# Attention and Fourier mixing on one core: new prices and smaller allowances in a planner

## The chip, the core and the metric

One of the eight cores of a Trainium2 chip runs the kernel. The metric is device time in microseconds (us) for one execution. The engines are TensorE (PE, matmuls; PEld, its weight loads), VectorE (DVE), ScalarE (ACT), GpSimd (POOL) and SyncE (SP, which here only issues DMAs). Each works through its own instructions in their written order and waits on semaphores for the others.

## The reference

Two independent parts, side by side in the output (2048 x 2048, fp32):

```python
# A: multi-head attention, S = 2048, D = 1024, 32 heads of 32
qkv = (x @ wqkv).reshape(B, S, 3, H, Dh).transpose(2, 0, 3, 1, 4)
scores = einsum("bhqd,bhkd->bhqk", q, k) * Dh ** -0.5
o = einsum("bhqk,bhkd->bhqd", softmax(scores), v)
a_out = o.transpose(0, 2, 1, 3).reshape(B, S, D) @ wo
# B: Fourier mixing by dense matrices, S = 2048, D = 1024
a = einsum("bsd,ed->bse", x, dft_hid_re);  b = einsum("bsd,ed->bse", x, dft_hid_im)
y = einsum("ts,bse->bte", dft_seq_re, a) - einsum("ts,bse->bte", dft_seq_im, b)
out = concatenate([a_out, y], axis=-1)
```

## The kernel before, in words

**Dense products (`fills`).** The projections of A and both steps of B are computed by a seven-product scheme on half-size blocks: each dense product is seven block products of sums and differences of blocks. The steps are `qkv` (A's projections), `dense1` and `dense2` (B), `project` (A's last product). An operand is loaded by SP (`fetch`, L380 for the first block, L389 for those added to it), summed on POOL or DVE (L396), and split by `halves` in a high part (a cast, L416 on ACT or L418 on DVE) and a low part (a subtraction, L421 on POOL or DVE). `group` then issues 12 or 24 matmuls (L332: high x high, low x high, high x low over 4 or 8 chunks) into one PSUM bank, and DVE evacuates the bank: in `qkv` L564 and L566, in the later steps L766 to L786. In `qkv`'s product 7 each group ends in two evacuations, each of which also adds a partial result `c` that SP loads back from DRAM (L643); partial results are stored there by L668 and L679. Sums used again are stored too: `sq_d`, `t1x_d` and others at L405. The fills have one fixed order. There are 6720 of them, 168 for each of the first five steps of `qkv`; product 7 is fills 1440 to 1727.

**Attention (`streams`).** For each head, stream S computes scores by rows (L1069, two matmuls into a double bank `psS`); DVE takes the negated row maximum (L1075), and ACT the exponentials with their sums (L1078). Stream T computes the transposed scores (L1201) with the maxima as further rows, and ACT writes their exponentials `pt` (L1205). Stream V multiplies four rows of `pt` with V (L1219: 16 products into a bank of `psD`, 32 PE instructions), and DVE adds them up in `ot` (L1230, L1232). Small products with `ident` (L1103, L1152) turn maxima and sums; `result` multiplies by the inverse sums (L1247, POOL or DVE).

**What sets the order.** At build time `Plan` plays the run through with a price for each operation, and every engine's instructions are written in the order in which the plan starts them. On the chip nothing of the plan's clock remains, only the orders. The main loop is PE's: at each moment it takes the next fill or the head of S, T or V, whichever is ready and ranks first; a head of a stream or the first matmul of a group must have been ready for `LATE` us. `others` starts what is ready on ACT, DVE, POOL and SP in order of rank; an operation with an `other` engine goes to whichever of the two is free first. The times:

```python
    def after(self, d, e, o):
        return d.end + (self.LAT_PE if e == "PE" else self.LAT) + self.SLACK.get((e, o.engine), 0.0)
...
                t = max(self.free[e], self.lane[0])
                self.dma = max(self.dma, t) + o.kb / o.lanes / self.KB_US
                o.end = self.dma + self.LANDING
```

So a transfer that SP starts to issue (price `ISSUE`, 0.46 us) is taken to move at `KB_US` KB per us behind all earlier ones, to land `LANDING` us later, and to be there for engine X another 0.1 + `SLACK[SP, X]` us later. `SLACK` thus keeps an engine from being given work that would make it stand and wait for a late transfer. `begin` holds SP back while `dma` is more than `QUEUE` ahead. A row-score operation costs 2 `MM`, a fill or transposed score `MM`, a product with V `SWITCH + 4 PV`.

Of the kernel before, what the change touches and what calls it, by code (L numbers as in the profile page):

```python
# [60 lines left out]
class Plan:  # L61
# [5 lines left out]
    LAT_PE = 0.2  # L67
    OVERLAP = {"ACT": 0.13, "DVE": 0.08, "POOL": 0.08}

    SLACK = {("SP", "POOL"): 2.0, ("SP", "DVE"): 2.5, ("SP", "PE"): 2.0, ("POOL", "DVE"): 0.7}  # L70
    KB_US = 340.0
    LANDING = 1.8
    QUEUE = 1.0

    def __init__(self):
# [37 lines left out]
    def after(self, d, e, o):  # L113
        return d.end + (self.LAT_PE if e == "PE" else self.LAT) + self.SLACK.get((e, o.engine), 0.0)

# [7 lines left out]
    def start(self, o, e=None):  # L123
# [4 lines left out]
        if o.kb:  # L128
            for _ in range(o.lanes):
# [3 lines that stand above are left out]
                self.lane = self.lane[1:] + [o.end]  # L133
# [52 lines left out]
def kernel(  # L186
# [90 lines left out]

    MM, PV, SWITCH, TINY = 0.232, 0.87, 0.34, 0.25  # L280
    ES, ET = 1.22, 0.61
    MAX, EVAC, CAST, BIT = 1.22, 0.69, 0.45, 0.27
    SUB = 1.34
    ISSUE = 0.46

    LATE = 0.3
    HB = 0
    ACAST = 0.6
    RES = 600
# [988 lines left out]
    while nf < len(fills) or any(place[n] < len(s) for n, s in streams.items()):  # L1278
# [18 lines left out]
        for n, (o, h, k) in heads.items():  # L1297
            if o.left:
                continue
            ready = o.ready + LATE  # L1300
            if n == "V":
# [4 lines left out]
            if n == "V":  # L1306

                near = any(m in heads and heads[m][0].left == 0 and heads[m][0].ready + LATE < pl.now + NEAR and not (m == "S" and held) for m in "ST")
                if (near or stock < STOCK) and pl.now < o.ready + PATIENCE:
# [14 lines left out]
        if nf < len(fills):  # L1324
            o, first, left = fills[nf]
            ready = o.ready if o.left == 0 else 1e18
            if first:
                ready = max(ready, room)
            if ready + (LATE if first else 0.0) <= pl.now:
                fill = o  # L1330
            elif ready < 1e17:
                times.append(ready + LATE)
        if fill is not None and (not ok or (not first and left <= HB) or nf / (FILL - RES) <= done / ATT):
# [56 lines left out]
```

## Time and profile before

| | |
|---|---|
| median of 3 runs | 3121.78 us (3120.04 to 3122.42) |
| the profiled execution | 3121.61 us |
| its span | 3119.8 us |
| granted clock of PE, mean | 0.994 |
| PE, DVE, ACT, POOL busy | 3066.8, 2503.5, 2299.1, 924.9 us |
| DMA | 567.77 MB, mean 182 GB/s |

The span runs from the first to the last instruction of the profiled execution; the time is taken outside it. Busy PE counts matmuls with their modelled ends, which overlap, so the distance from one start to the next tells more than the duration of one. The waits name the engine and tile that ended an idle time. In a row of a stretch the columns are its length, the busy us (and instructions) of each engine, the granted clock, the DMA share and GB/s.

### The profile page before, as it was taken

What the parts mean: (1) busy time and instruction counts of PE and PEld (TensorE: products, weight loads), DVE (VectorE), ACT (ScalarE), POOL (GpSimd) and SP (SyncE); (2) the same over time, 40 slices, a digit from 0 to 9 for tenths busy, and PEclk for the clock granted to TensorE, in tenths of its full rate; (3) what the DMA queues carried; (4) which work ended last, traced back from release to release, by engine and by line L of the source; (5) the groups of instructions that cost most, each with busy time, mean ns of one, the idle gap of its engine ahead of it and who ended that gap; (6) DMA issues with size and microseconds to landing.
All of it is one profiled execution on the core that took longest, in us unless ns stands there. A gap on an engine that the chain in (4) does not pass through costs nothing.

```text
span 3119.8 us, 45400 instructions
## 1 busy us (share of the span) xinstructions
PE 3066.8 (98%) x15040; PEld 2151.0 (69%) x15040; DVE 2503.5 (80%) x3182; ACT 2299.1 (74%) x4316; POOL 924.9 (30%) x683
## 2 busy tenths in 40 slices
PE   9899999899999999999999999999999999999999
PEld 7687666566666666666676666666666666666787
DVE  6669888878777878887777798888877888887886
ACT  4237888778888888888888878888888887775321
POOL 3423323412112321122111253323211244433443
PEclk9999999999999999999999999999999999999999
DMA  9975557876634544464433576445433467546952
GB/s 333 326 241 192 184 159 246 291 233 217 182 86 145 190 132 155 135 189 147 133 126 104 180 241 195 146 148 173 141 115 98 141 213 232 159 150 206 330 172 91
DMA packets 359673, 567.77 MB, mean 182 GB/s; under 512 B 86640, under 2 KB 88176, under 8 KB 359440
## 3 DMA queue, kind: packets, MB, share of 16 engines
q1 hardware_dynamic: 359440, 564.87, 56.8%
q8 instruction: 121, 1.98, 0.3%
q14 instruction: 112, 0.92, 0.1%
HBM read 407.70 MB, written 156.50 MB: 181 GB/s over the span
## 4 chain that ended last, share of the span: by engine, by line
PE 66%; DVE 6%; ACT 1%; issue 1%; DMA 0%; POOL 0%; SPq 0%; ACTq 0%; DVEq 0%; POOLq 0%
PE pd L332 29%; PE psT L1201 12%; PE pd L1219 11%; PE psS L1069 11%; PE psT L332 3%; DVE negm L1075 2%; ACT psS L1078 1%; DVE raw L396 1%; DVE h L418 1%; DVE slot L421 1%; DVE l L421 0%; DVE slot L770 0%; DVE slot L418 0%; DVE e L781 0%; PE psS L1152 0%
## 5 line engine op out<-in xcount | busy, mean ns | idle before, releaser
L1075 DVE TENSOR_REDUCE negm<-psS 128x1 f32<-128x1024 f32 x1024 | 1231.9, 1217 | 206.2 <-PE psS L1069 202.4
L1205 ACT ACTIVATE pt<-psT 128x512 f32<-128x512 f32 x2048 | 1155.4, 627 | 322.0 <-PE psT L1201 315.7
L1078 ACT ACTIVATE psS<-psS,negm 128x1024 f32<-128x1024 f32 x1024 | 1146.6, 1120 | 187.0 <-DVE negm L1075 179.9
L332 PE MATMUL pd<-slot,h 128*128 128x512 f32 x3336 | 1157.8, 397 | 3.2 <-DVE ot L1232 1.7
L1201 PE MATMUL psT<-qs,ks 98*128 98x512 f32 x2048 | 822.4, 405 | 5.1 <-ACT pt L1205 4.2
L332 PEld LDWEIGHTS pd<-slot,h 128*128 128x128 f32 x3336 | 632.4, 190 | 156.9 <-issue 12.6
L332 PE MATMUL pd<-slot,l 128*128 128x512 f32 x1668 | 661.5, 397 | 0.8 <-POOL l L421 0.8
L1201 PEld LDWEIGHTS psT<-qs,ks 98*128 98x128 f32 x2048 | 385.9, 189 | 193.2 <-issue 65.6
L1069 PE MATMUL psS<-ks,qs 96*128 96x512 f32 x1552 | 479.0, 399 | 12.1 <-ACT psS L1078 11.1
L1219 PE MATMUL pd<-pt,vt 128*32 128x512 f32 x4096 | 470.9, 601 | 4.5 <-DVE c L564 2.6
L421 POOL TENSOR_TENSOR l<-raw,h 128x512 fp32r<-128x512 f32 x174 | 233.1, 1339 | 798.5 <-DVE h L418 407.7
L396 POOL TENSOR_TENSOR raw<-raw,g 128x512 f32<-128x512 f32 x229 | 307.9, 1348 | 422.6 <-DVE raw L396 102.4
L332 PEld LDWEIGHTS pd<-slot,l 128*128 128x128 f32 x1668 | 316.7, 190 | 76.0 <-issue 5.7
L1069 PEld LDWEIGHTS psS<-ks,qs 96*128 96x128 f32 x1552 | 289.3, 189 | 95.2 <-ACT psS L1078 30.4
L1219 PEld LDWEIGHTS pd<-pt,vt 128*32 128x32 f32 x4096 | 121.2, 110 | 283.6 <-issue 262.1
L421 POOL TENSOR_TENSOR slot<-raw,slot 128x512 fp32r<-128x512 f32 x131 | 182.2, 1396 | 396.6 <-DVE slot L418 319.0
L1078 ACT ACTIVATION_READ_ACCUMULATOR psS<-psS,negm 128x1 f32 x1024 | 242.0, 236 | 0.0
L332 PE MATMUL pd<-slot,slot 128*128 128x512 f32 x768 | 195.9, 393 | 0.0
L1232 DVE TENSOR_TENSOR ot<-ot,pd 128x512 f32<-128x512 f32 x96 | 65.8, 686 | 134.6 <-PE pd L1219 134.5
L332 PEld LDWEIGHTS pd<-slot,slot 128*128 128x128 f32 x768 | 145.0, 189 | 32.2 <-issue 0.4
L418 DVE CAST h<-raw 128x512 fp32r<-128x512 f32 x305 | 153.4, 503 | 15.8 <-PE pd L332 13.8
L421 DVE TENSOR_TENSOR slot<-raw,slot 128x512 fp32r<-128x512 f32 x153 | 156.4, 1025 | 6.0 <-ACT slot L416 2.4
(114 smaller groups left out, 2093.5 us busy)
## 6 DMA issues: line engine op xcount, KB each, us to landing
raw<-in_ct SPq DMA_DIRECT2D x224, 256.0 KB, 3.4
g<-in_ct SPq DMA_DIRECT2D x128, 256.0 KB, 3.5
c<-u_d SPq DMA_DIRECT2D x104, 256.0 KB, 3.6
qk_d<-e SPq DMA_DIRECT2D x52, 512.0 KB, 3.8
qs<-qk_d SPq DMA_DIRECT2D x128, 192.0 KB, 3.7
ks<-qk_d SPq DMA_DIRECT2D x128, 192.0 KB, 2.7
raw<-ab_d SPq DMA_DIRECT2D x96, 256.0 KB, 2.9
g<-ab_d SPq DMA_DIRECT2D x80, 256.0 KB, 3.6
```

The lines of the kernel that those rows point to most:

```text
L332: nc.tensor.matmul(box["ps"], a[1]((a[0].hi, a[0].lo)[u]()), b[1]((b[0].hi, b[0].lo)[v]()), start=k == 0, stop=k == n - 1)
L396: (nc.gpsimd if e == "POOL" else nc.vector).tensor_tensor(out=dest(), in0=dest() if a is None else a.get(), in1=other["q"] if "q" in other ...
L418: nc.vector.tensor_copy(hi(), raw())
L421: (nc.gpsimd if e == "POOL" else nc.vector).tensor_tensor(out=lo(), in0=raw(), in1=f(hi()), op=ALU.subtract)
L1069: nc.tensor.matmul(p[:, i * NB : i * NB + NB], (qx["t"] if own else QS[h % 2][0:96])[:, qt * P : qt * P + P], KS[h % 2][0:96, c * 1024 + i ...
L1075: nc.vector.tensor_reduce(out=ST["negm"][:, c, qt : qt + 1], in_=box["p"], axis=AX.X, op=ALU.max, negate=True)
L1078: nc.scalar.activation(box["p"], box["p"], AF.Exp, bias=ST["negm"][:, c, qt : qt + 1], accum_out=ST["sums"][:, c, qt : qt + 1])
L1201: nc.tensor.matmul(box["p"], KS[h % 2][0:98, t * P : t * P + P], QS[h % 2][0:98, j * NB : j * NB + NB], start=True, stop=True)
L1205: nc.scalar.activation(box["t"], box["p"], AF.Exp)
L1219: nc.tensor.matmul(po["p"][j * DH : j * DH + DH, :], VT[h][:, k, :], box["t"], start=(k == t + 1 - PVB), stop=(k == t), tile_position=(0, ...
L1232: nc.vector.tensor_tensor(out=po["o"], in0=po["o"], in1=po["p"], op=ALU.add)
```

## The change

Five prices of the plan and three allowances get new values. `KB_US` rises, `LANDING` falls, and the slack for a transfer falls to 1.5 us for POOL, DVE and PE; the price of a matmul rises slightly, that of one row of a product with V falls and that of starting such a product rises (together 3.82 us before, 3.668 after); `LATE` rises. No operation, buffer or dependency changes.

```diff
-    SLACK = {("SP", "POOL"): 2.0, ("SP", "DVE"): 2.5, ("SP", "PE"): 2.0, ("POOL", "DVE"): 0.7}
-    KB_US = 340.0
-    LANDING = 1.8
+    SLACK = {("SP", "POOL"): 1.5, ("SP", "DVE"): 1.5, ("SP", "PE"): 1.5, ("POOL", "DVE"): 0.7}
+    KB_US = 380.0
+    LANDING = 1.6
...
-    MM, PV, SWITCH, TINY = 0.232, 0.87, 0.34, 0.25
+    MM, PV, SWITCH, TINY = 0.234, 0.762, 0.62, 0.25
...
-    LATE = 0.3
+    LATE = 0.35
```

## The prediction

> **What bounds the kernel now.** I read the busy shares first, then what TensorE (PE) waited for, then the stretches in which it waited, then the engine that kept it waiting.
>
> ```profile
> span 3119.8 us, 45400 instructions
> PE 3066.8 (98%) x15040; PEld 2151.0 (69%) x15040; DVE 2503.5 (80%) x3182; ACT 2299.1 (74%) x4316; POOL 924.9 (30%) x683
> ```
>
> PE is busy for 98%, and both versions issue the same 15040 matmuls, so only what PE loses can change. From start to start, two neighbouring matmuls of 512 columns lie 231 to 237 ns apart (medians by pair of kinds). Summing what each distance has above its median, PE loses 92 us in the whole run: 19.3 between 0 and 200 us, 21.4 between 500 and 700, 36 between 700 and 2800, and the rest at 200 to 500 and in the end. That is all that any order could win. The waits of PE:
>
> ```profile
> PE psS L1069 <- ACT psS L1078: 13.9, 24, 1.3
> PE psT L332 <- ACT h L416: 8.3, 1, 8.3
> PE psT L332 <- ACT slot L416: 6.0, 1, 6.0
> PE psT L1201 <- ACT pt L1205: 4.2, 3, 3.6
> ```
>
> (total, times, longest, in us.) The 6.0 is the start of the run, before any data is there; both versions have it. The one wait of 8.3 ends at 111.53. The queue of SyncE (SP) and PE around it:
>
> ```profile
> 94.46 3.45 SPq L405 DMA_DIRECT2D sq_d<-er  x1
> ...
> 100.86 0.49 SPq L380 DMA_DIRECT2D er<-in_wqk  x1
> ...
> 103.53 1.60 SPq L389 DMA_DIRECT2D raw<-in_wqk  x2
> ```
> ```profile
> 102.82 0.39 PE L332 MATMUL psT<-slot,h 128*128 128x512 f32 x1
> 111.53 0.80 PE L332 MATMUL psT<-slot,h 128*128 128x512 f32 x1 [8.32 <-ACT h L416]
> ```
>
> The weight piece that PE wants at 102.8 is a sum of three loads, and SP has issued the last of them only at 105.1, because they stand behind a store that SP itself waited 3.45 us for. Short waits cost a second time:
>
> ```profile
> 97.15:100.57 3.42, 3.42 (x10) 2.65 (x9) 1.62 (x3) 0.63 (x1) 0.00 (x0) 0.50 1.16 328
> 107.39:117.63 10.24, 6.10 (x14) 4.50 (x15) 5.88 (x8) 2.52 (x4) 3.51 (x3) 0.50 1.03 387
> 540.90:544.30 3.40, 3.40 (x10) 2.63 (x10) 2.32 (x3) 3.40 (x7) 0.61 (x1) 0.50 0.92 336
> ```
>
> (stretch, length, then PE, weight loads, DVE, ACT, POOL; granted clock; DMA share; GB/s.) The clock 0.50 in these stretches doubles the distance of matmuls; it follows a stretch of some 3.4 us in which PE was busy for about two thirds or less.
>
> **The change, part by part.** No instruction is added or removed. Five prices and three allowances of the planner change, so the written order changes on every engine. In the built programs 50 operations more stand on DVE (3182 to 3232), 47 fewer on POOL (683 to 636), 3 fewer on ACT; PE and SP keep their counts.
>
> *The head.* In SP's order the last load of that weight piece goes from place 125 to 120, and behind the store that blocked until 97.9 it is the 4th issue, not the 11th. Seven issues at 0.45 to 0.8 us (the rows above) are 3.2 to 5.6; I take 5, which agrees with 1.5 MB less queued ahead of it (33.5 to 32.0) at about 0.32 MB/us. So the wait of 8.3 becomes 3.3. In the 10.24 us at half clock PE was busy 6.10, of which it lost half, 3.05; one stretch of 3.4 at half clock would remain, 1.7 lost. Together -5 - 1.3 = **-6.3**. Ends: 0, if the store blocks longer, and -11.4 (8.3 + 3.05). The waits of 1.40 and 0.84 us at 94 to 96 stay: their piece has 28.2 MB ahead of it in both orders. Next late could be the piece of group 42 (39.8 MB ahead, moved by about 130 us); PE gets there at 142 before and 136 after, so it is covered.
>
> The Trainium skill (TensorE: Matmul & The Clock Gate, "Why this matters for your kernels") asks for no PE gaps over about 3 us if the clock is to be kept. The trace is stricter: the half clock at 540.90 follows waits of only 0.45 and 0.59 us. By the skill's rule a wait cut to just under 3 us would cost no clock, and the sum would be 1.7 us lower; by the rows it still costs.
>
> *The stretch at 526 to 636 us.* Each fill group here ends in two evacuations, and DVE is 82 to 94% busy, often slowed by POOL:
>
> ```profile
> 601.19 0.42 DVE L418 CAST e<-e 128x512 fp32r<-128x512 f32 x1
> ...
> 601.86 1.85 DVE L418 CAST slot<-raw 128x512 fp32r<-128x512 f32 x2
> 603.63 1.78 DVE L421 TENSOR_TENSOR l<-raw,h 128x512 fp32r<-128x512 f32 x1
> ```
>
> (a cast takes 0.42 alone, 0.9 beside POOL; a subtraction 0.69 alone, here 1.78.) Between the same two evacuations, twelve groups apart, the order holds on DVE 119 operations before and 112 after (row maxima 38 and 31). At 1.217 a maximum, 0.68 an evacuation, 0.6 a cast and 0.85 a subtraction that is 100.7 and 92.3 us of DVE, beside 85.8 and 79.0 us of PE work: DVE is short by 14.9 and 13.3. The 21.4 us lost make 1.44 per us of shortage, so the gain is 2.3 if the attention work taken out finds no room elsewhere and 12 (8.4 x 1.44) if it finds it for nothing; I take **-6**. Against it: the evacuations need the `c` loads, which landed after 4.1 us in the median; the plan now allows 4.33 from the issue (0.46 + 256/380 + 1.6 + 0.1 + 1.5), not 5.61 (0.46 + 256/340 + 1.8 + 0.1 + 2.5). Of 31 such loads 14 took longer than 4.33, by 8.3 us in all, and one longer than 5.61. The load is often hidden behind its group's matmuls, so between 0 and 8.3: **+2**. Queued behind such a late evacuation are the next row maxima, and ACT's exponentials and PE's scores wait for those.
>
> *The middle, 700 to 2800.* DVE's additional work: 47 operations x 0.69 + 3 = 35 us, less what POOL no longer slows. Beside POOL, DVE's casts, subtractions and sums took 189 us more than at their undisturbed means, 0.20 per us of POOL; 64 us less of POOL give back 13. Net 22 us, 0.7% of the span. PE's loss by DVE's share comes from two stretches, 1400:1800 (76% DVE, 4.4 us lost) and 1800:2200 (86%, 9.5): 0.13 us per 100 us and point. Over 2150 us: **+2** (0 to 4).
>
> *Late loads.* A load to POOL was allowed 5.11 us from its issue and is now allowed 4.33. Between 650 and 2800, 69 of 779 loads took over 5.11 (30.0 us beyond it in all) and 160 over 4.33 (113.8 beyond). DVE waited for loads 3.8 us in 700 to 2800 before; 3.8 times as much is 10.6 more. DVE idles a fifth of the time, so I let a quarter reach PE: **+3**. Ends: 0, and +30 (PE's whole 10.8 us of waits there times 2.8). If DVE's idle time were not there, all of it would fall on the score matmuls.
>
> *`LATE` 0.3 to 0.35.* 253 starts lie 60 to 130 ns above their median, 27 us. With 50 ns more allowance PE takes other ready work first: 0 to -12.7 (253 x 0.05); most of these have no other ready work, so a quarter: **-3**. The new prices of a product with V (16 matmuls: 0.62 + 4 x 0.762 = 3.67; the trace 3.70; before 3.82) and of a matmul (0.234; the trace 0.231 to 0.237) remove an error of at most 0.12 us per operation between PE and the others, which all wait by semaphore: 0.
>
> Sum: -6.3 - 6 + 2 + 2 + 3 - 3 = -8.3. The profiled execution took 3121.61 (span 3119.8 and 1.8 around it), 0.2 below the median of the runs, so 3121.6 - 8.3 = **3113**. A measurement of this kernel tells some 0.2% (6.2 us) from no change.
>
> **The rivals.** *Late loads hold DVE (slower).* One mechanism: DVE stands at a load in the middle stretch, the row maxima behind it come late. Price +30 instead of +3: 3140. It decides the sign once more than 21% of the 83.8 us of new overshoot reaches PE (17.5 us). For it: the DMA share is 0.44 to 0.61 there and loads still vary from 2.5 to 6.4 us. Against it: DVE waited only 3.8 us for loads in 2100. Chance 0.18.
>
> *The load phase is paced by the rate (slower).* In the first 160 us the queues moved 323 to 341 GB/s, 53 MB; the planner reckoned 340 and now 380, so its clock runs ahead by 53/0.340 - 53/0.380 = 16 us, DVE stands at loads while evacuations wait behind it, and the head loses up to 16 rather than winning 6.3: 3136. For it: DMA share 0.95 to 1.03. Against: PE's own order is nearly fixed there. Chance 0.08. The Trainium skill (DMA: Bandwidth & Descriptors, "Specifications") gives about 358 GB/s of HBM per core, which speaks against 380; the trace shows 387 in the 10 us above, but nothing over 341 in a stretch of 30 us or more.
>
> *The win is given back (same).* DVE stays as short at 526 to 636 as it was, and the head's 5 us are waited for at a later group: -6.3 + 6 - 1 = about -1, 3120. Chance 0.22.
>
> *Both stretches come free (faster).* Head -11.4, the 500 to 700 loss all gone (-21.4): 3089. Chance 0.1. That the change does nothing is excluded: hardly a stretch of the orders is alike.
>
> **How the numbers follow.** The forecast has 0.42: faster 0.42 + 0.1 = 0.52; same 0.22; slower 0.26. The range leaves out the lowest of the free case and the dearest late loads: 3095 to 3136.
>
> **What would show it.** Right: the wait near 111 at 2 to 5 us; less than 16 us lost at 500 to 700; DVE busy near 2525, POOL near 861; DVE's waits for loads in 700 to 2800 under 15 us. Wrong: PE losing over 50 us in 700 to 2800 with DVE waiting for DMAs, or a head wait as long as before.

## The result, and the profile after

The changed kernel takes 3130.21 us in the median of 10 runs (3127.45 to 3138.48); the kernel before, beside it, 3122.1 (3118.09 to 3123.55). The ratio is 1.0032 with a 95% interval of 1.0023 to 1.0042: slower by 8 us by the medians, where 8 us less were forecast. Its profiled execution took 3128.93 us, 7.3 more than that of before. The first lines of its page:

```profile
span 3127.0 us, 45415 instructions
PE 3070.1 (98%) x15040; PEld 2138.3 (68%) x15040; DVE 2537.1 (81%) x3232; ACT 2310.7 (74%) x4313; POOL 865.9 (28%) x636
```

The engines' sums came out nearly as worked out (DVE 2537 for 2525, POOL 866 for 861). PE has the same 15040 matmuls; what grew is the time that it loses between them. PE's waits (total, times, longest, in us):

```profile
PE psS L1069 <- ACT psS L1078: 12.9, 20, 1.5
...
PE psS L1069 <- DMA ks<-qk_d: 4.8, 2, 2.9
...
PE psT L332 <- ACT h L416: 0.2, 1, 0.2
```

The wait of 8.3 us for the weight piece (`ACT h`) is gone; the 0.2 us left on that line lies at 2953.98, in the end of the run. In its place PE waits for a transfer itself, twice, for the first block of `ks`; no such line stood in the profile before. And there is a new stretch of losses near the end (stretch, length, then PE, weight loads, DVE, ACT, POOL; clock; DMA share; GB/s), first before, then after:

```profile
2900.00:3000.00 100.00, 100.00 (x440) 82.32 (x439) 91.81 (x110) 29.54 (x49) 49.38 (x33) 1.00 0.90 308
```
```profile
2900.00:3000.00 100.00, 93.29 (x402) 74.62 (x401) 85.92 (x98) 27.64 (x46) 51.60 (x34) 1.00 0.83 289
```

440 matmuls ran there before, 402 after. The same measure as in the prediction (start-to-start distances of matmuls beyond the median of their pair of kinds, products with V left out inside) gives PE's loss by stretch:

| us | 0-200 | 200-500 | 500-700 | 700-2800 | 2800-2900 | 2900-3000 | 3000-end |
|---|---|---|---|---|---|---|---|
| before | 19.3 | 8.4 | 21.4 | 36.5 | 2.3 | 0 | 4.3 |
| after | 17.1 | 15.0 | 16.0 | 38.5 | 5.0 | 8.6 | 2.6 |
| difference | -2.2 | +6.6 | -5.4 | +2.0 | +2.7 | +8.6 | -1.7 |

Together +10.6. Inside the products with V, which the measure leaves out, distances sum to 391.4 us after and 395.1 before, -3.7; the two make 6.9 of the span's 7.2.

**What happens at 2900 to 3000.** Attention has just ended, PE works through fills alone, and the queues are full: the DMA share is 1.00 at 355 GB/s from 2900 to 2950. The first sum of that kind on DVE in the kernel before, then DVE, POOL and PE in the changed kernel:

```profile
2941.89 5.79 DVE L396 TENSOR_TENSOR s<-s,g 128x512 f32<-128x512 f32 x4
```

```profile
2939.12 1.51 DVE L396 TENSOR_TENSOR s<-s,g 128x512 f32<-128x512 f32 x2 [2.31 <-DMA g<-o_d]
...
2951.45 1.89 DVE L396 TENSOR_TENSOR t<-t,g 128x512 f32<-128x512 f32 x2 [2.27 <-DMA g<-in_wo]
```
```profile
2950.90 1.29 POOL L396 TENSOR_TENSOR t<-t,g 128x512 f32<-128x512 f32 x1 [3.47 <-DMA g<-in_wo]
...
2954.44 1.46 POOL L421 TENSOR_TENSOR l<-raw,h 128x512 fp32r<-128x512 f32 x1
```
```profile
2942.84 0.50 PE L332 MATMUL pd<-slot,l 128*128 128x512 f32 x1 [1.19 <-DVE l L421]
...
2955.96 0.50 PE L332 MATMUL psT<-slot,l 128*128 128x512 f32 x1 [1.48 <-POOL l L421]
2960.01 0.50 PE L332 MATMUL psT<-slot,l 128*128 128x512 f32 x1 [1.07 <-DVE l L421]
```

DVE stands for 2.3 us before a sum whose load has not landed; the kernel before comes to these sums 5 us later and does not stand. The sum belongs to the projection, whose first matmul starts at 2962.6. Behind it in DVE's order stand the evacuations (`e`) and low parts (`l`) that PE needs next, and PE waits for those. POOL does the same: it stands 3.5 us at a load, and the low part that it makes afterwards is the one that PE waits 1.48 us for. (POOL stands at loads in the kernel before too, some 15 us from 2880 to 3000 against 16 here; what counts is whether a part that PE needs next stands behind such a load.) With two waits for DVE's evacuations into `slot` at 2975 and 2979 (1.5 and 0.9 us) and three short ones, PE's named waits are 6.8 of the 8.6 us lost. By the planner's rule a sum starts no earlier than the plan has its load ready, so the plan had these loads there sooner than they came.

**What happens at 72.** SP issued the first load of `ks` at 64.96 before and at 69.04 after (its place in SP's order moved from 83 to 90), and PE came to it at 69.9, where it had come at 72.58 before:

```profile
72.77 0.50 PE L1069 MATMUL psS<-ks,qs 96*128 96x512 f32 x1 [2.86 <-DMA ks<-qk_d]
75.21 1.65 PE L1069 MATMUL psS<-ks,qs 96*128 96x512 f32 x3 [1.93 <-DMA ks<-qk_d]
```
```profile
74.64:81.46 6.82, 6.25 (x15) 4.90 (x16) 3.04 (x3) 2.96 (x5) 2.62 (x3) 0.50 1.03 321
```

4.8 us of waits and 6.82 us at half clock, of which PE was busy 6.25, so another 3.1: this takes back most of the 11.4 that the vanished wait had cost.

### The profile page after: what moved, and what is told of

Same layout as the page of the kernel before. It is cut to its first block, busy times and chain, and to the rows that moved or that the text cites. A ratio compares the mean times of both kernels' runs of the same rounds, so it can differ in the third digit from the quotient of the medians.

```text
span 3127.0 us, 45415 instructions
## 1 busy us (share of the span) xinstructions
PE 3070.1 (98%) x15040; PEld 2138.3 (68%) x15040; DVE 2537.1 (81%) x3232; ACT 2310.7 (74%) x4313; POOL 865.9 (28%) x636
## 4 chain that ended last, share of the span: by engine, by line
PE 77%; DVE 11%; DMA 6%; issue 2%; ACT 2%; SPq 1%; POOL 1%; ACTq 0%; DVEq 0%; POOLq 0%
PE pd L332 33%; PE psT L1201 14%; PE psS L1069 14%; PE pd L1219 13%; DVE negm L1075 3%; PE psT L332 3%; ACT psS L1078 1%; DVE slot L421 1%; DVE slot L418 1%; DMA raw<-in_ct 1%; DVE raw L396 1%; DMA raw<-in_xa 1%; DVE l L421 1%; DVE h L418 1%; DMA er<-in_xa 1%
## 5 line engine op out<-in xcount | busy, mean ns | idle before, releaser
L1069 PE MATMUL psS<-ks,qs 96*128 96x512 f32 x1552 | 479.9, 400 | 17.9 <-ACT psS L1078 12.3
L421 POOL TENSOR_TENSOR l<-raw,h 128x512 fp32r<-128x512 f32 x143 | 194.0, 1356 | 983.4 <-DVE h L418 342.7
L396 POOL TENSOR_TENSOR raw<-raw,g 128x512 f32<-128x512 f32 x218 | 294.1, 1353 | 526.8 <-issue 74.0
L421 POOL TENSOR_TENSOR slot<-raw,slot 128x512 fp32r<-128x512 f32 x138 | 192.9, 1403 | 321.9 <-DVE slot L418 179.6
L1078 ACT ACTIVATION_READ_ACCUMULATOR psS<-psS,negm 128x1 f32 x1024 | 230.8, 225 | 0.0
L1069 PE MATMUL psS<-ks,qx 96*128 96x512 f32 x496 | 153.3, 401 | 2.1 <-DVE l L1111 1.3
```

Of the source, the lines that this page charges most:

```text
L396: (nc.gpsimd if e == "POOL" else nc.vector).tensor_tensor(out=dest(), in0=dest() if a is None else a.get(), in1=other["q"] if "q" in other ...
L421: (nc.gpsimd if e == "POOL" else nc.vector).tensor_tensor(out=lo(), in0=raw(), in1=f(hi()), op=ALU.subtract)
L1069: nc.tensor.matmul(p[:, i * NB : i * NB + NB], (qx["t"] if own else QS[h % 2][0:96])[:, qt * P : qt * P + P], KS[h % 2][0:96, c * 1024 + i ...
L1078: nc.scalar.activation(box["p"], box["p"], AF.Exp, bias=ST["negm"][:, c, qt : qt + 1], accum_out=ST["sums"][:, c, qt : qt + 1])
```

## The experiments

Theory R: the new transfer allowances promise loads too early where the queues are full, and that is the loss. Rival P: the new prices and `LATE` cost. Rival O: any reshuffle of the orders costs this much. Each run is timed beside the kernel before on the same chip. The losses in a stretch are from one profiled execution each, which can lie some us from the median (run 1: 3126.97, run 6: 3121.25, run 12: 3108.73). OLD stands for KB_US 340, LANDING 1.8, SLACK 2.0/2.5/2.0 (POOL, DVE, PE), NEW for 380, 1.6, 1.5/1.5/1.5.

**1. The old allowances for the end alone.**

```diff
 # on the changed kernel
         if not heads:
             att_on[0] = False
+            pl.KB_US, pl.LANDING, pl.SLACK = 340.0, 1.8, {OLD}
```

> The changed kernel, but the planner goes back to the three old transfer allowances (KB_US 340, LANDING 1.8, the old SLACK) once attention is written out, so the order is that of the changed kernel up to about 2770 us. Theory R (loads promised too early where the queues are full): the 8.6 us that PE loses between 2900 and 3000 us fall to 2 or less, DVE's 6.6 us of waits for loads from 2880 to 3060 fall to about 1, and the time to about 3121. Rival O (any reshuffle of the order costs about as much, somewhere): that stretch still loses 5 us or more, time 3125 to 3133. Rival P (the new prices and LATE are what costs): no change, 3129.

Measured: 3122.16 us, ratio 1.0008 (0.9999 to 1.0017). PE's loss at 2900 to 3000 is 0.6 us, not 8.6, although everything up to the end of attention is ordered as in the changed kernel (by line and tile, SP's order first differs at 2898, DVE's at 2905 and PE's nowhere):

```profile
2950.00:3000.00 50.00, 49.67 (x218) 40.38 (x217) 48.98 (x58) 12.21 (x20) 31.34 (x20) 1.00 0.77 253
```

(In the changed kernel that half of the stretch had 44.87 us of PE and 191 matmuls.) Undoing the three transfer allowances for the last tenth of the run removes the slowdown.

**2. The mirror image.** The kernel before, with NEW set at the same place.

> The mirror image: the kernel before, with the three new transfer allowances only once attention is written out. Theory R: PE loses about 8 us between 2900 and 3000 us where it lost none, with DVE or POOL standing at loads of weights and of o_d; time about 3129. Rival O: between 0 and 8 us, with no link to loads. Rival P: 3122, as before.

Measured: 3128.66 us, ratio 1.0029 (1.0019 to 1.004). 5.9 us lost at 2900 to 3000, where the kernel before lost none, and again PE waits for low parts behind a DVE that stands 4.3 us at `g<-o_d`:

```profile
PE psT L332 <- DVE l L421: 1.8, 1, 1.8
PE psT L332 <- POOL l L421: 1.6, 1, 1.6
```

The two runs together show that the allowances in this one stretch are enough to make the 8 us, and that taking them back there is enough to remove them.

**3. All transfer allowances, without prices and `LATE`.** The kernel before with NEW throughout.

> The kernel before with the transfer allowances alone changed in the whole run (KB_US 380, LANDING 1.6, SLACK 1.5); the prices and LATE are the old ones. Theory R: all of the loss is here: 3128 to 3133, with waits of PE for the first ks load near 72 us and 6 us or more lost between 2900 and 3000 us. Rival P: 3122 or below. Rival O: anywhere from 3118 to 3133, the losses spread without a link to loads.

Measured: 3133.69 us, ratio 1.0039 (1.0027 to 1.0051), just above what theory R allowed. As it has it: waits for `ks` 4.5 us, 6.2 us lost at 2900 to 3000. What it had not named: 51.6 us are lost between 700 and 2800 (36.5 before), where DVE stands 34.4 us at loads (3.8 before).

**4. Prices and `LATE` alone.** The changed kernel with OLD throughout.

> The kernel before with the prices of matmul and product with V and LATE 0.35 alone; the transfer allowances are the old ones. Theory R: the prices are worth nothing or a few us: 3113 to 3122, no loss between 2900 and 3000 us, no wait for the first ks load. Rival P: 3129. Rival O: 3118 to 3133, spread.

Measured: 3124.44 us, ratio 1.0014 (1.0005 to 1.0022). No loss at 2900 to 3000 (0.1), no wait for `ks`, as R said, but a little slower than before instead of faster: rival P has a part.

**5 and 6. Rate or slack?** The changed kernel with one of the two put back.

```diff
 # 5: e5_rate_old
-    KB_US = 380.0
-    LANDING = 1.6
+    KB_US = 340.0
+    LANDING = 1.8
 # 6: e6_slack_old
-    SLACK = {("SP", "POOL"): 1.5, ("SP", "DVE"): 1.5, ("SP", "PE"): 1.5, ...}
+    SLACK = {("SP", "POOL"): 2.0, ("SP", "DVE"): 2.5, ("SP", "PE"): 2.0, ...}
```

> The changed kernel with KB_US 340 and LANDING 1.8 again, SLACK at the new 1.5. Theory R1 (it is the rate: with the queues full, the plan's clock for transfers runs ahead by 380 against the 355 to 360 GB/s that the trace shows, and the error adds up over 50 us): PE loses 2 us or less between 2900 and 3000 us (8.6 in the changed kernel), time 3119 to 3124. Theory R2 (it is the smaller slack): still 5 us or more there, 3127 to 3131.

> The changed kernel with the old SLACK (2.0, 2.5, 2.0), KB_US 380 and LANDING 1.6 as changed. Theory R1: half to one us more slack does not cover an error that adds up: 5 us or more lost between 2900 and 3000 us, 3126 to 3131. Theory R2: 2 us or less there, 3119 to 3123.

Measured: with the old rate and the new slack 3118.65 us, ratio 0.999 (0.9981 to 0.9999), 0.8 us lost at 2900 to 3000 and no wait for `ks`. With the new rate and the old slack 3125.12 us, ratio 1.0013 (1.0005 to 1.0022), 5.2 us lost there and this line:

```profile
PE psS L1069 <- DMA ks<-qk_d: 5.1, 2, 3.3
```

Both times lie a little below what R1 gave. Both marks, the loss at 2900 to 3000 and the wait for `ks`, stay with the new rate (with its landing time) and go with the old one: the old slack does not cover the rate's error. But it is not without effect: with it 5.2 instead of 8.6 us are lost there, and the whole run is some 4 us slower than before, not 8. The units matter here: a tile of 128x512 fp32 is 256 KB to the planner and 262144 bytes, so its 340, 360 and 380 KB per us are 348, 369 and 389 GB/s. Over the 50 us from 2900 on, in which the changed kernel moved 355 GB/s, a plan at 389 runs ahead by 50 x (1 - 355/389) = 4.4 us and one at 348 by nothing (an estimate; the plan also holds SP back, which it leaves out).

**7. More slack for PE's own loads.** The changed kernel with OLD at the end, as in 1, and `("SP", "PE"): 6.0` before it.

> The changed kernel with the old transfer allowances once attention is written out (as in e1_tail_old) and, before that, a slack of 6.0 us for loads that PE itself uses (SP to PE, 1.5 in the change). Theory R: PE no longer stands at the first ks loads at 72 to 76 us (5.2 us, and some 3 more at half clock, in the changed kernel); 0 to 100 us loses 5 us or less instead of 11, and the wait for the third weight piece near 111 us comes back at 2 to 5 us; time 3117 to 3120. Rival: the first scores only wait elsewhere, 3122 as e1_tail_old.

Measured: 3159.78 us, ratio 1.0131 (1.0115 to 1.0146), far from both expectations. The waits for `ks` shrink to 0.8 us, but the slack holds for `ks`, `qs` and V of all 32 heads, and attention ends at 2944 us instead of 2893, with 864 fills left after it instead of 954. PE waits 25 times for ACT's `pt` (9.9 us), and 25 us are lost at 2900 to 3000, where the last transposed scores stand alone; run 9 shows the same more plainly.

**8. A control for the reshuffle.** The kernel before with `ISSUE = 0.465` instead of 0.46.

> A control: the kernel before with the price of issuing a transfer at 0.465 instead of 0.46 us, which changes no allowance worth the name but reshuffles the orders. Theory R: 3119 to 3125, no loss between 2900 and 3000 us. Rival O (any reshuffle costs about as much as the change): 3126 to 3133.

Measured: 3122.92 us, ratio 1.0004 (0.9995 to 1.0012), 0.6 us lost at 2900 to 3000. A new order by itself need not cost 8 us, and run 10 is a second one that does not. With run 1, which keeps the changed kernel's order up to the end and loses the slowdown, that leaves little of rival O.

**9. `LATE` alone.** The kernel before with `LATE = 0.35`.

> The kernel before with LATE 0.35 instead of 0.3 alone. The prediction's step: 3 us won, 3119, and fewer starts of PE that lie 60 to 130 ns above their median (253 before). Rival (LATE does nothing but reshuffle): 3119 to 3125, about as many such starts.

Measured: 3136.8 us, ratio 1.0045 (1.0032 to 1.0057): slower than the whole change by its ratio, though the intervals overlap. Late starts of 60 to 130 ns do not become fewer (281; 265 before by the same count). What grows is the loss at 2900 to 3000, from nothing to 12.6 us, and it comes from the balance between fills and attention. After the last product with V the kernel before has 953 fills left, this one 864 (dense matmuls from there to the end, in this run):

```profile
2919.70:3135.80 216.10, 203.56 (x864) 165.18 (x864) 0.98 0.51 173
```

864 is the least there can be: the last 192 fills of `dense2` and the 672 of `project` share buffers and inputs with attention (`behind`), and wait for all of its results. By the rule of the main loop, a head of a stream that must have been ready for longer loses PE to a fill more often (argued from the code, not counted); in any case the other fills were used up while attention still ran: the fill that is the first one left after attention in the kernel before, at 2892.9, starts at 2873.0 here. PE then had nothing but transposed scores, at ACT's pace:

```profile
2911.56 0.98 PE L1201 MATMUL psT<-qs,ks 98*128 98x512 f32 x2 [0.51 <-ACT pt L1205]
2912.76 0.99 PE L1201 MATMUL psT<-qs,ks 98*128 98x512 f32 x2 [0.21 <-ACT pt L1205]
```
```profile
2880.00:2940.00 60.00, 53.11 (x250) 33.52 (x249) 29.79 (x44) 28.23 (x51) 4.91 (x4) 0.91 0.58 195
```

6.9 us idle and a clock of 0.91 in these 60 us. The changed kernel does not pay this: it has 954 fills left, with prices and `LATE` alone 917. That the other new numbers make up for it is seen in these counts; which of them does it was not tested.

**10 and 11. Slack alone, rate alone.** The kernel before with `SLACK` 1.5 for all three, and the kernel before with `KB_US = 380.0`.

> The kernel before with SLACK 1.5 for all three, KB_US 340 and LANDING 1.8 as before. Theory R1 (the rate costs, the slack does not): 3116 to 3122, 2 us or less lost between 2900 and 3000 us, PE does not stand at ks loads. Rival R2: 3126 or more.

> The kernel before with KB_US 380 alone. Theory R1: the loss of the stretch with full queues is here: 4 us or more between 2900 and 3000 us and a wait of PE for the first ks loads of 3 us or more, 3125 to 3131. Rival R2: 3119 to 3123, neither of them.

Measured: slack alone 3121.43 us, ratio 0.9999 (0.999 to 1.0008), 1.6 us lost at 2900 to 3000 and 0.4 us of waits for `ks`. Rate alone 3124.14, ratio 1.0008 (0.9999 to 1.0017), 7.2 us lost there and 3.6 us of waits for `ks`. Both marks go with the rate, here without the landing time. The total is below the 3125 to 3131 expected, and its interval takes in no change at all: the third weight piece (a wait of 4.6 us instead of 8.3) and the stretch at 500 to 700 (17.2 us) gave a part back. So the rate makes the loss at the end; as a change of its own its cost to the whole run is not shown.

**12. A rate between the two.** The changed kernel with `KB_US = 360.0` (369 GB/s) and `LANDING = 1.8`.

> The changed kernel with KB_US 360 and LANDING 1.8, SLACK 1.5: the rate that the queues reached at a DMA share of 1.00. Theory R1: between e5_rate_old (0.8 us lost between 2900 and 3000 us) and the changed kernel (8.6): 1 to 5 us there, 3118 to 3125. If the plan must only not run ahead of the measured rate: 2 us or less there and 3115 to 3120.

Measured: 3115.09 us, ratio 0.9976 (0.9966 to 0.9987): faster than before by 0.24%, and below what R1 gave. Against 340 (run 5, ratio 0.999) the intervals overlap. The profiled execution is the fastest of its eight, so the losses below are on the low side. Its stretches:

```profile
0.00:160.00 160.00, 147.69 (x629) 120.03 (x630) 110.00 (x140) 60.26 (x100) 56.75 (x45) 0.99 1.00 345
2900.00:2950.00 50.00, 48.96 (x213) 39.38 (x212) 40.42 (x44) 17.49 (x31) 27.26 (x19) 1.00 1.00 350
```

3.8 us are lost at 2900 to 3000, between 0.8 and 8.6 as R1 expected; but in the first 200 us only 11.6, where before lost 19.3 and the changed kernel 17.1. In these three executions the head does best in the middle: at 340 SP's order brings the weight pieces late (5.9 and 5.4 us of waits in run 5), at 380 `ks` (4.8), at 360 each is short:

```profile
PE pd L332 <- ACT h L416: 2.7, 1, 2.7
...
PE psS L1069 <- DMA ks<-qk_d: 1.8, 1, 1.8
PE psT L332 <- ACT h L416: 1.7, 1, 1.7
```

## Why the prediction was wrong

**The missing term: the end.** The sum had nothing for 2800 to 3060. Measured are +8.6 us at 2900 to 3000, the largest difference of all, and runs 1 and 2 show that it comes from the transfer allowances there; +2.7 us at 2800 to 2900 stay in run 1 (5.5 lost) and are not explained. The mechanism was in the text, as the rival "the load phase is paced by the rate" at a chance of 0.08, but tied to the first 160 us, the only part whose queue rows were read for it. The sentence that nothing over 341 GB/s stands in a stretch of 30 us or more does not hold outside the stretches that it went by: the kernel before moved 369 GB/s from 5 to 35 us, and 360 from 2900 to 2950 at a DMA share of 1.00, so the end is as full as the head. The step that failed is the choice of place: the rival should have been asked of every stretch with a full queue. Its ground against ("PE's own order is nearly fixed there") does not help at the end: PE's order there is the same in the changed kernel and in run 1, but DVE's is not, and a DVE that stands at a load holds the evacuations and low parts that the fixed order needs next. The measured time lies inside the stated range only because the range took in slower rivals; the sum itself pointed the other way.

**The head: -6.3 forecast, -2.2 measured.** The reading of SP's order was right: the weight piece was worked out to wait 3.3 us, and where only the transfers change (run 3) it waits 2.8; in the changed kernel PE comes to it later still, at 105.95, and does not wait. What was left out is the other end of the same move. What goes to the back of SP's order when weight loads go forward is `ks`, seven places later, and PE's first scores stand on it. The order shows that as plainly; only the piece that was late before was looked up.

**526 to 636: -4 forecast, -5.4 measured (500 to 700).** Right in size. That the reason is DVE's shortage was not tested by a run of its own; of the other orders seven lose between 12.3 and 17.2 us there and four, runs 2 and 7 to 9, 19.0 to 20.8. Run 1, in the same order as the changed kernel up to there, loses 19.1, so one execution tells such a term to some 3 us.

**The middle: +2 by more work on DVE, +3 for late loads, -3 for `LATE`; +2.0 measured.** The sum is right by luck, since two of its terms are not. DVE's waits for loads rose by 24.5 us (3.8 to 28.3), not 10.6, and PE's named waits there did not rise. So far DVE's idle time did cover, better than the quarter allowed for. But run 3 has 34.4 us of such waits and 15 us more loss of PE, so the cover is no constant; what makes the difference between these two is open. The rate alone hardly raises them (4.7 in run 11), the slack alone does (16.0 in run 10). The term of -3 for `LATE` has the wrong sign as a thing by itself: run 9 loses 14 us. The prediction priced `LATE` by starts that come a little late, and never asked what PE takes instead: a fill, which the end of the run then lacks.

**200 to 500: nothing forecast, +6.6 measured.** Only the changed kernel and run 1, which has its order up to there, lose 15 and 16 us; the twelve other orders, before among them, 8.2 to 12.4. Runs 4 to 6 take back the allowances together, the rate or the slack, run 3 the prices with `LATE`, and in none of them does it stay (10.0 to 11.2 us); so no one of these groups brings it alone, and why stays open.

**The rate.** From 2900 to 2950 the queues moved 345 to 379 GB/s wherever the DMA share was 0.99 to 1.04. The planner's 380 KB per us, 389 GB/s, is above all of these, its 340 (348 GB/s) near the lowest; of three rates tried with the new slack, prices and `LATE`, 380 (with the new landing time) is the slowest, and 360 is ahead of 340 by less than their intervals tell apart. The Trainium skill (DMA: Bandwidth & Descriptors, "Specifications") gives a limit of about 358 GB/s of HBM per core. The trace lies on both sides of it, up to 379, so as a limit the measurement does not bear it out, while as a warning against 380 it was right.

**Clock.** The prediction held against the rule of the Trainium skill (TensorE: Matmul & The Clock Gate, "Why this matters for your kernels"), no PE gaps over about 3 us, that shorter waits are followed by half clock too. That showed again at 74.64, after a wait of 2.86 us, half a microsecond of work and the first 1.4 of the next wait's 1.93 us.

## What to carry to other kernels

Choose a planner's rate for transfers by what the queues move when they are full, in the same units: here 389 GB/s, above all that was measured over 50 us, hardly raised DVE's waits where the queues were half idle (run 11), but at the full end of the run its error added up, and half to one us more slack did not cover it. When one load is seen to move forward in an issuing order, look up which load moves back, and who waits for that one. Ask of a mechanism that you find in one stretch where else in the run its condition holds; a table of the queue's share by stretch would have shown both ends of this run at once.

## What the runs showed of the hardware

DVE, idle a fifth of the time and bound to its written order, hid 24 us of additional waits for loads over 2100 us, with 2 us more of PE's loss; the same engine at the end, 86 to 92% busy, with only fills behind it, stood 7.0 us at loads, and PE lost 8.6. The queues' rate at a full share was not one number: 345 to 379 GB/s in the same 50 us of different orders. And the changed kernel's runs scatter more, 11 us from lowest to highest against 5.5 before.
